# Two causal blocks instead of four in an FFT convolution that runs beside a feed-forward layer

## The chip, the cores and the metric

The kernel runs on one core of a Trainium2 chip. The metric is the device time of one execution in microseconds (us). TensorE multiplies matrices into PSUM; VectorE (DVE), ScalarE (ACT) and GpSimd (POOL) work elementwise, and GpSimd works from SBUF alone in this kernel; SyncE (SP) issues nearly all DMAs.

## The reference, cut to what matters

```python
# x, v: (2, 12480, 128)   pos_emb: (12480, 64)   w_in: (128, 2048)   w_out: (2048, 128)
h = (relu(pos_emb @ w1) @ w2) * exp(-0.01 * pos)      # the filter, one per channel
u = x * v
y = irfft(rfft(u, n=2*S, axis=1) * rfft(h, n=2*S, axis=0), n=2*S, axis=1)[:, :S]   # causal convolution
z = (x * y).reshape(24960, 128)
a = z @ w_in
out = maximum(0.01 * a, a) @ w_out
```

## The kernel before, in words

The sequence is cut into NBLK = 4 causal blocks of 3136 tokens. A *unit* (b, j) is block j of batch b; the eight units run in the order (0,0), (1,0), (0,1), (1,1), and so on to (1,3). Batch 0 also carries the filter: its units transform 64 more channels (`hid`), so they do more work.

Each unit has a **forward stage** (`ConvA`) and an **inverse stage** (`ConvB`). The forward stage loads tokens, multiplies x by v on GpSimd (`prep`, L198), makes a first Fourier step on TensorE (`burst`, L224), copies PSUM to SBUF (ACT, L169; only in the first unit half of them on DVE, L646) and stores that to DRAM (`scr1`). The inverse stage goes through chunks of frequencies (NCH = 7 per unit): it loads a chunk (`bin`), makes the second Fourier step (`up`, L400; `ep` L352 and `hp` L381 for the filter), multiplies spectra, sums the products into `pin`, and transforms back (`dp`, L436) into `scr2`. `up` and `burst` share one PSUM buffer of two banks (`cv`) once the feed-forward layer runs, so each use of `cv` waits until the elementwise engine has emptied it.

Block j of the output needs the products of block spectra u(i)·g(j-i). With half-shifted spectra in this kernel, block j costs 1, 2, 5 and 2 chunk products for j = 0, 1, 2, 3 (`first` runs on DVE from PSUM, L416; `rest` runs on GpSimd from SBUF, L416 too; `join`, L424 to L426, adds and subtracts them on GpSimd, for j = 2 partly on DVE). That makes ten per batch. Both engines' products use the same two buffers `t0` and `t1`.

The **feed-forward layer** runs in 52 tiles of up to 490 tokens. A tile has 16 steps; a step is three matmuls with `w_in` (`m1`, L765 to L767), ACT and DVE work that makes two parts of the activation (`rh` L771, `rl` L772), and three matmuls with `w_out` (`m2`, L789 to L792). In front of a tile stand `front` calls (L744 `yp`, DVE `zt` L746, transposes): they finish the convolution for 4 token groups and make z. There are 64 of them.

The first unit (0,0) runs alone, before the layer starts, mixed with the unpacking of the weights (`wprep`, a generator that is advanced 4 or 3 times per step of `ConvB`). We call that part the **head**. Every engine takes its instructions in the order of the program. The order after the head is set by `pace`: each unit gets a window of feed-forward steps, sized by the table `cost`, and the pieces of its two stages are spread evenly over the window:

```python
cost = [0, 80, 110, 110, 215, 215, 125, 125]      # weight of each unit after the first
self.rest = {0: [], 1: [(u(0), g(1), "y")], 3: [(u(0), g(3), "y")],
             2: [(u(1), g(1), "y"), (u(1), g(2), "p"), (u(0), g(2), "y")]}[j]
```

Units must be done before the first `front` that needs them. Tiles after the last unit use another activation path (`k >= LEAKY`) that has three matmuls fewer per tile and more ACT and DVE work.

## Time and profile before

| | |
|---|---|
| time, median of 3 runs | 2028.54 us (2026.91 to 2029.88) |
| profiled execution, its own time | 2025.03 us |
| its span, first to last instruction | 2023.2 us |
| TensorE busy | 1760.4 us, 87% |
| VectorE, ScalarE, GpSimd busy | 45%, 40%, 45% |
| mean granted TensorE clock | 0.949 |
| DMA | 290.54 MB, mean 144 GB/s |

TensorE is the busiest engine by far. The 45% of GpSimd is a mean over the whole span, and its work is bunched: in the forty slices of the page it is at 7 to 8 tenths in some slices and at 1 or 2 in others. The granted clock is the share of full speed (2.4 GHz) that TensorE was given; the lower of its two levels is half of that, so a mean of 0.9 over a stretch says that it had the lower level for a fifth of the stretch.

### The profile page before, as it was taken

Reading aid. Unit: us, or ns where it says so; the run is one execution under the profiler, and the core shown is the slowest. Engines: PE = TensorE matmul, PEld = TensorE weight load, DVE = VectorE, ACT = ScalarE, POOL = GpSimd, SP = SyncE. Lnnn points to the kernel's source line nnn. Section 1 sums busy time; section 2 is a strip of 40 time slices with the busy share of each in tenths; the row PEclk is TensorE's granted clock in tenths of the full one; section 3 lists DMA queues with packets and bytes.
Section 4 is the critical chain, followed back from the end, with each engine's and each line's share of the span. In section 5 each row is a group of like instructions: output and inputs, shape, how many; then the busy total and the mean of one; then the engine's idle time right before and its main releaser. Section 6 shows DMA issues by size and latency. Waiting matters only on the chain.

```text
span 2023.2 us, 27361 instructions
## 1 busy us (share of the span) xinstructions
PE 1760.4 (87%) x9932; PEld 1302.7 (64%) x9932; DVE 901.2 (45%) x1435; ACT 819.1 (40%) x1459; POOL 901.6 (45%) x608
## 2 busy tenths in 40 slices
PE   3765989978998899787889878789989999999999
PEld 2433846755675577555568656567766687668888
DVE  3763443333443434433444444444333444445665
ACT  1222534533453354232235323234543354335666
POOL 4221121157418610888772388882148622860000
PEclk9976989999999999888989998899999999999999
DMA  6547664566565555354335443333556355631110
GB/s 147 161 135 235 177 194 137 141 236 209 151 182 192 175 146 176 122 162 133 126 89 132 148 145 132 117 99 103 145 193 223 112 144 171 192 115 56 40 32 16
DMA packets 203935, 290.54 MB, mean 144 GB/s; under 512 B 26503, under 2 KB 135017, under 8 KB 203605
## 3 DMA queue, kind: packets, MB, share of 16 engines
q1 hardware_dynamic: 200098, 286.57, 46.8%
q10 hardware_dynamic: 3703, 2.24, 0.6%
q8 instruction: 78, 1.28, 0.3%
q14 instruction: 56, 0.46, 0.1%
HBM read 181.23 MB, written 107.51 MB: 143 GB/s over the span
## 4 chain that ended last, share of the span: by engine, by line
PE 58%; POOL 20%; DVE 8%; issue 7%; DMA 3%; ACT 2%; SPq 1%; ACTq 0%; POOLq 0%; DVEq 0%
POOL t L416 10%; PE mh L765 8%; PE mh L767 6%; PE mh L766 6%; PE acc L790 6%; PE acc L792 6%; PE acc L789 6%; PE cv L224 4%; POOL t L424 4%; PE cv L400 4%; DVE t L416 3%; PE cv L436 3%; PE yp L744 2%; POOL pin L425 2%; POOL pin L426 2%
## 5 line engine op out<-in xcount | busy, mean ns | idle before, releaser
L772 DVE SCALAR_TENSOR_TENSOR rl<-mh,rh 128x490 fp32r<-128x490 f32 (+3 forms) x704 | 458.8, 662 | 603.7 <-ACT rh L771 601.7
L771 ACT ACTIVATE rh<-mh 128x490 fp32r<-128x490 f32 (+3 forms) x704 | 406.4, 579 | 503.1 <-PE mh L767 483.7
L765 PE MATMUL mh<-zh,w_in_h 128*128 128x490 f32 (+4 forms) x832 | 367.1, 441 | 66.9 <-DVE rl L772 66.2
L766 PE MATMUL mh<-zl,w_in_h 128*128 128x490 f32 (+4 forms) x832 | 323.4, 389 | 0.0
L767 PE MATMUL mh<-zh,w_in_l 128*128 128x490 f32 (+4 forms) x832 | 323.2, 389 | 0.0
L790 PE MATMUL acc<-rl,w_out_h 128*128 128x490 f32 (+4 forms) x832 | 321.8, 387 | 0.0
L789 PE MATMUL acc<-rh,w_out_h 128*128 128x490 f32 (+4 forms) x832 | 321.0, 386 | 0.0
L792 PE MATMUL acc<-rh,w_out_l 128*128 128x490 f32 (+4 forms) x832 | 320.9, 386 | 0.0
L765 PEld LDWEIGHTS mh<-zh,w_in_h 128*128 128x128 f32 x832 | 161.5, 194 | 195.1 <-DVE rl L772 92.0
L425 POOL TENSOR_TENSOR pin<-t,t 128x512 f32<-128x512 f32 (+1 forms) x112 | 142.4, 1272 | 258.8 <-DVE t L416 250.8
L416 DVE TENSOR_TENSOR t<-cv,sp 128x1024 f32<-128x1024 f32 (+1 forms) x126 | 133.8, 1103 | 112.0 <-POOL pin L426 67.8
L416 POOL TENSOR_TENSOR t<-sp 128x1024 f32<-128x1024 f32 (+1 forms) x84 | 178.1, 2141 | 9.6 <-issue 6.9
L767 PEld LDWEIGHTS mh<-zh,w_in_l 128*128 128x128 f32 x832 | 161.8, 194 | 27.4
L789 PEld LDWEIGHTS acc<-rh,w_out_h 128*128 128x128 f32 x832 | 161.7, 194 | 26.7
L792 PEld LDWEIGHTS acc<-rh,w_out_l 128*128 128x128 f32 x832 | 160.8, 193 | 26.5
L790 PEld LDWEIGHTS acc<-rl,w_out_h 128*128 128x128 f32 x832 | 160.3, 193 | 27.0 <-DVE rl L780 0.2
L766 PEld LDWEIGHTS mh<-zl,w_in_h 128*128 128x128 f32 x832 | 163.5, 196 | 13.5 <-DVE zl L758 0.3
L198 POOL TENSOR_TENSOR t<-pp,ct 113x512 f32<-113x512 f32 x28 | 36.1, 1290 | 202.5 <-PE cv L224 93.1
L400 PE MATMUL cv<-bin,mb 128*64 128x512 f32 (+1 forms) x416 | 109.4, 638 | 17.2 <-ACT hs L386 12.6
L416 POOL TENSOR_TENSOR t<-sp,hs 128x1024 f32<-128x1024 f32 (+1 forms) x56 | 118.8, 2143 | 7.4 <-issue 4.6
L436 PE MATMUL cv<-pin,mi 64*128 64x512 f32 (+1 forms) x416 | 109.3, 631 | 14.2 <-DVE t L416 13.1
L424 POOL TENSOR_TENSOR t<-t,pin 128x1024 f32<-128x1024 f32 (+1 forms) x56 | 119.5, 2134 | 0.0
(123 smaller groups left out, 1886.3 us busy)
## 6 DMA issues: line engine op xcount, KB each, us to landing
sp<-g SPq DMA_DIRECT2D x72, 512.0 KB
cin<-scr SPq DMA_DIRECT2D x64, 392.0 KB
scr<-ct SPq DMA_DIRECT2D x96, 256.0 KB
sp<-u SPq DMA_DIRECT2D x48, 512.0 KB
scr<-sp SPq DMA_DIRECT2D x64, 294.0 KB
bin<-scr SPq DMA_DIRECT2D x24, 768.0 KB
scr<-sp SPq DMA_DIRECT2D x32, 392.0 KB
g<-hs SPq DMA_DIRECT2D x24, 512.0 KB
```

Source lines behind the costliest of these rows:

```text
L400: nc.tensor.matmul(p[64 * jo:64 * jo + 64, ri, :w].rearrange("p (k d) -> p k d", d=D), mb[:, ri, :], t[:, jo * h:jo * h + h, self.off:], s ...
L416: eng.tensor_tensor(out=t[i], in0=u[:R, :, :w], in1=g[:R, i:i + 1, :w].to_broadcast([R, 2, w]), op=ALU.mult)
L424: G(out=t[0], in0=t[0], in1=init[:R, :, :w], op=ALU.add)
L425: G(out=acc[:R, 0, :w], in0=t[0][:, 0], in1=t[1][:, 1], op=ALU.subtract)
L765: nc.tensor.matmul(hp, w_in_h[:, fs], zh, start=True, stop=False)
L766: nc.tensor.matmul(hp, w_in_h[:, fs], zl, start=False, stop=False)
L767: nc.tensor.matmul(hp, w_in_l[:, fs], zh, start=False, stop=True)
L771: nc.scalar.activation(out=rh, in_=hp, func=AF.Relu)
L772: nc.vector.scalar_tensor_tensor(out=rl, in0=hp, scalar=0.0, in1=rh, op0=ALU.max, op1=ALU.subtract)
L789: nc.tensor.matmul(ap, w_out_h[:, f, :], rh, start=(f == 0), stop=False)
L790: nc.tensor.matmul(ap, w_out_h[:, f, :], rl, start=False, stop=False)
L792: nc.tensor.matmul(ap, w_out_l[:, f, :], rh, start=False, stop=last and k >= LEAKY)
```

## The change

The sequence is cut into two blocks of 6272 tokens. A block has twice as many rows in the forward transform; these are paired with their neighbours half a block apart, so that the transform matrices stay as small as before and a sum and a difference (a radix-2 butterfly) join the two halves. Four things follow.

- The forward stage ends a burst with one ACT copy of one half and two DVE operations (sum, difference) instead of one ACT copy of both halves. A unit has twice as many bursts.
- An inverse chunk covers 4 frequencies of both halves instead of 8 of one. A unit has 13 chunks instead of 7. Block 0 costs one product and block 1 two, three per batch. DVE's products get buffers of their own (`sp3` and `pp`), GpSimd keeps `t0` and `t1`.
- Before a `front`, GpSimd joins the two halves of `cin` (`join_front`, two operations of 98x512). The table `gt` of the last inverse step, formerly resident in SBUF, is loaded for each front into a ring of two.
- There are four units. The first one, still in the head, is twice as large. `wprep` starts later in the forward stage and is advanced 3 or 2 times per step in the inverse stage. `cost` has three entries.

```diff
-NBLK = 4
+NBLK = 2
-BLK = KA * NM
+BLK = KA * NB
-KC = 8
+KC = 4
...
             def burst(self, c, i0, n):
...
-                self.evac(turn[0], o, a[:, :, :n * e].rearrange("k w (i e) -> k w i e", e=e))
+                a1 = cpt("a1s", 512, 2)[:2 * KA, :n * e]
+                nc.scalar.copy(a1, a[:, 1, :n * e])
+                a0, a1 = (t.rearrange("k (i e) -> k i e", e=e) for t in (a[:, 0, :n * e], a1))
+                nc.vector.tensor_tensor(out=o[:, :, 0, :], in0=a0, in1=a1, op=ALU.add)
+                nc.vector.tensor_tensor(out=o[:, :, 1, :], in0=a0, in1=a1, op=ALU.subtract)
...
-                self.first = [(g(0), "y")] + ([(g(1), "p")] if j == 2 else [])
-                self.rest = {0: [], 1: [(u(0), g(1), "y")], 3: [(u(0), g(3), "y")],
-                             2: [(u(1), g(1), "y"), (u(1), g(2), "p"), (u(0), g(2), "y")]}[j]
-                self.loads = [("p", b)] if j == 3 else []
+                self.first = [(g(0), "y")]
+                self.rest = [] if j == 0 else [(u(0), g(1), "y")]
+                self.loads = []
...
-                if self.j < 2:
+                if self.j == 0:
                     us = self.tile("us", 1024).rearrange("p (r w) -> p r w", r=2)
                     nc.scalar.copy(us[:R, :, :w], p[:R, :, :w])
...
-            def t01(self, c):
+            def t01(self, c, fresh):
                 R, w = self.dims(c)
-                return [cpt(f"t{i}", 1024).rearrange("p (r w) -> p r w", r=2)[:R, :, :w] for i in range(2)]
+                t = (spt(3), cpt("pp", 1024)) if fresh else (cpt("t0", 1024), cpt("t1", 1024))
+                return [i.rearrange("p (r w) -> p r w", r=2)[:R, :, :w] for i in t]
...
         def load_front(t):
...
+            g = gr()
+            for r in range(2):
+                nc.sync.dma_start(out=g[KA * r:KA * r + KA, :NI * 2 * KA].rearrange("k (i n) -> k i n", n=2 * KA),
+                                  in_=cg[:KA, m0 % 32:m0 % 32 + NI, r, m0 // 32, 0, :])
...
+        def join_front(t):
+            c, g, xt = mlp_in[t]
+            cj = fr.tile([128, 2, NI, D], F32, tag="cj", name="cj", bufs=1)[:2 * KA]
+            eng = nc.gpsimd if t else nc.vector
+            for p, op in ((0, ALU.add), (1, ALU.subtract)):
+                eng.tensor_tensor(out=cj[:, p], in0=c[:, :, 0, :], in1=c[:, :, 1, :], op=op)
+            mlp_in[t] = cj, g, xt
...
-                load_t(NI, 16 - NI, (nc.sync, nc.scalar))
+                load_t(NI, 32 - NI, (nc.sync, nc.scalar))
...
-                for _ in range(4 if i < 7 else 3):
+                for _ in range(3 if i < 7 else 2):
                     next(wprep, None)
...
-        cost = [0, 80, 110, 110, 215, 215, 125, 125]
+        cost = [0, 220, 310, 290]
...
         for t in range(1, total):
+            at(ends[t] - 7, "join", t)
             at(ends[t] - 3, "front", t)
             at(ends[t], "front", t)
```

**DVE in the forward stage of unit (1,0).** This is VectorE's queue at the start of the feed-forward layer (`rl` is the layer's own work, `zt` and `zl` belong to a front, `cv` is the PSUM of a burst). Before:

```order
L772 SCALAR_TENSOR_TENSOR rl<-mh,rh 128x392 x2
L746 TENSOR_TENSOR zt<-yp,xm_108 113x512
L772 SCALAR_TENSOR_TENSOR rl<-mh,rh 128x392 x3
L758 TENSOR_TENSOR zl<-zp,zh 128x392
L772 SCALAR_TENSOR_TENSOR rl<-mh,rh 128x392 x5
L746 TENSOR_TENSOR zt<-yp,xm_107 113x512
```

Now:

```order
L792 SCALAR_TENSOR_TENSOR rl<-mh,rh 128x392 x5
L756 TENSOR_TENSOR zt<-yp,xm_90 113x512
L237 TENSOR_TENSOR sp<-cv,a1s 98x4x128
L238 TENSOR_TENSOR sp<-cv,a1s 98x4x128
L792 SCALAR_TENSOR_TENSOR rl<-mh,rh 128x392 x3
L778 TENSOR_TENSOR zl<-zp,zh 128x98
L778 TENSOR_TENSOR zl<-zp,zh 128x294
L792 SCALAR_TENSOR_TENSOR rl<-mh,rh 128x392 x2
```

The two rows on `cv` and `a1s` are the butterfly. They are new on DVE, and the PSUM buffer is free for TensorE's next use only after the second.

**GpSimd in an inverse chunk.** Before, one chunk of unit (1,2), the block with five products (`sp` are loaded spectra, `t_` are `t0` and `t1`, `pin` and `pp` are the two sums):

```order
L425 TENSOR_TENSOR pin<-t_9154,t_9155 128x512
L426 TENSOR_TENSOR pin<-t_9154,t_9155 128x512
L425 TENSOR_TENSOR pp<-t_9215,t_9216 128x512
L426 TENSOR_TENSOR pp<-t_9215,t_9216 128x512
L416 TENSOR_TENSOR t_9237<-sp 128x1024
L416 TENSOR_TENSOR t_9238<-sp 128x1024
L424 TENSOR_TENSOR t_9237<-t_9237,pin 128x1024
L425 TENSOR_TENSOR pin<-t_9237,t_9238 128x512
L416 TENSOR_TENSOR t_9292<-sp 128x1024
L416 TENSOR_TENSOR t_9293<-sp 128x1024
L424 TENSOR_TENSOR t_9292<-t_9292,pp 128x1024
L425 TENSOR_TENSOR pp<-t_9292,t_9293 128x512
```

Four more rows of the same kind (a third product) follow before the next chunk. Now, one chunk of unit (1,1), the second of its thirteen, and the join that follows it:

```order
L438 TENSOR_TENSOR pin<-sp,pp 128x512
L439 TENSOR_TENSOR pin<-sp,pp 128x512
L429 TENSOR_TENSOR t_11459<-sp 128x1024
L429 TENSOR_TENSOR t_11460<-sp 128x1024
L437 TENSOR_TENSOR t_11459<-t_11459,pin 128x1024
L438 TENSOR_TENSOR pin<-t_11459,t_11460 128x512
L439 TENSOR_TENSOR pin<-t_11459,t_11460 128x512
L584 TENSOR_TENSOR cj<-cin 98x512 x2
```

A unit of batch 0 has two operations of 128x256 more in each chunk. The join `cj` is new in this queue, behind whatever of the chunk is not yet done.

**SyncE at a front.** The loads of one front before:

```order
L566 DMA cin<-scr_01_70 98x2x512
L95 DMA xm_107<-in_x_dram 48x512 x2
L98 DMA xm_107<-in_x_dram 2x512
```

And now:

```order
L569 DMA cin<-scr_10_65 98x1024
L573 DMA gt_94<-in_cg_dram 49x4x98 x2
L92 DMA xm_90<-in_x_dram 48x512 x2
L95 DMA xm_90<-in_x_dram 2x512
```

The two `gt` loads are new in SP's queue at each of the 64 fronts.

## Rows read from the trace of the kernel before

**Rows 1.** Windows by stage: sum, busy per engine, granted clock, DMA share, GB/s

```profile
core 0: us, PE busy (x) PEld busy (x) DVE busy (x) ACT busy (x) POOL busy (x), PEclk, DMA share, GB/s
0.00:192.80 192.80, 104.83 (x643) 62.65 (x643) 98.28 (x183) 45.12 (x79) 58.43 (x64) 0.87 0.58 163
192.80:255.00 62.20, 62.20 (x400) 51.40 (x401) 25.35 (x43) 28.71 (x50) 7.65 (x6) 0.92 0.67 192
255.00:325.00 70.00, 59.51 (x250) 34.32 (x250) 28.25 (x36) 26.07 (x42) 15.86 (x14) 0.93 0.59 181
325.00:395.00 70.00, 65.91 (x411) 50.24 (x411) 26.90 (x45) 33.97 (x61) 10.28 (x8) 1.00 0.52 141
395.00:525.00 130.00, 109.96 (x738) 75.17 (x735) 45.68 (x63) 52.00 (x84) 81.90 (x58) 0.96 0.63 206
...
590.00:702.00 112.00, 98.04 (x457) 64.24 (x457) 46.49 (x67) 42.43 (x72) 76.37 (x49) 0.97 0.60 192
...
795.00:1055.00 260.00, 206.70 (x1155) 148.65 (x1154) 107.86 (x159) 80.73 (x144) 204.55 (x122) 0.89 0.42 131
...
1125.00:1375.00 250.00, 205.90 (x932) 151.84 (x931) 114.27 (x172) 78.12 (x144) 195.34 (x108) 0.90 0.38 119
...
1480.00:1610.00 130.00, 118.04 (x788) 80.36 (x785) 52.43 (x73) 48.39 (x83) 99.96 (x70) 0.99 0.55 181
...
1695.00:1815.00 120.00, 112.37 (x554) 79.79 (x551) 55.83 (x82) 43.16 (x79) 91.57 (x56) 0.97 0.51 159
1815.00:2023.20 208.20, 201.41 (x1107) 172.03 (x1106) 124.98 (x231) 129.45 (x255) 0.00 (x0) 1.00 0.13 37
```

**Rows 2.** Waits of DVE in the inverse stage of unit (1,1): total us, times, longest

```profile
DVE t L416 <- POOL pin L426: 30.2, 6, 6.7
```

**Rows 3.** Timeline of TensorE in the head: start us, duration us

```profile
32.98 1.60 PE L224 MATMUL cv<-t,tt 49*98 49x192 f32 x8
37.74 1.60 PE L224 MATMUL cv<-t,tt 49*98 49x192 f32 x8
69.22 4.52 PE L224 MATMUL cv<-t,tt 49*98 49x192 f32 x24
94.43 3.27 PE L400 MATMUL cv<-bin,mb 128*64 128x512 f32 x8
154.54 3.68 PE L400 MATMUL cv<-bin,mb 128*64 128x512 f32 x8
163.91 1.94 PE L400 MATMUL cv<-bin,mb 128*64 128x512 f32 x8
192.76 0.69 PE L765 MATMUL mh<-zh,w_in_h 128*128 128x392 f32 x1 [0.57 <-ACT zh L757]
```

**Rows 4.** Groups of instructions by line: count, busy us, mean ns, idle before

```profile
L416 POOL TENSOR_TENSOR t<-sp 128x1024 f32<-128x1024 f32 (+1 forms) x84 | 178.1, 2141 | 9.6 <-issue 6.9
L425 POOL TENSOR_TENSOR pin<-t,t 128x512 f32<-128x512 f32 (+1 forms) x112 | 142.4, 1272 | 258.8 <-DVE t L416 250.8 <-PE mh L767 2.5
L416 DVE TENSOR_TENSOR t<-cv,sp 128x1024 f32<-128x1024 f32 (+1 forms) x126 | 133.8, 1103 | 112.0 <-POOL pin L426 67.8 <-ACT us L404 31.6 <-PE cv L400 10.9
L169 ACT COPY sp<-cv 98x768 f32<-98x768 f32 (+1 forms) x80 | 70.9, 886 | 74.5 <-PE cv L224 68.7 <-DMA scr<-sp 3.2 <-DMA out_dram<-os 1.8
L746 DVE TENSOR_TENSOR zt<-yp,xm 113x512 f32<-113x512 f32 x64 | 44.1, 689 | 35.8 <-PE yp L744 33.7 <-DMA e<-es 0.4 <-DMA hs<-in_v_dram 0.4
L400 PE MATMUL cv<-bin,mb 128*64 128x512 f32 (+1 forms) x416 | 109.4, 638 | 17.2 <-ACT hs L386 12.6 <-ACT hs L388 3.7 <-DVE t L416 1.0
L436 PE MATMUL cv<-pin,mi 64*128 64x512 f32 (+1 forms) x416 | 109.3, 631 | 14.2 <-DVE t L416 13.1 <-POOL pin L425 1.0
L224 PE MATMUL cv<-t,tt 49*98 49x128 f32 (+3 forms) x1024 | 104.1, 336 | 2.0 <-ACT pts L207 1.2 <-DVE t L213 0.6
L381 PE MATMUL cv<-w,esg 64*64 64x128 f32 x588 | 25.4, 296 | 0.0
L352 PE MATMUL cv<-mb,bin 128*64 128x128 f32 x294 | 25.0, 312 | 45.6 <-issue 41.8 <-DMA bin<-scr 2.3 <-DVE t L416 1.5
```

More of the change, by code (lines that the diff above doesn't have):

```diff
@@ L166, in __init__ @@
                 self.off = self.e - D
-                self.granules = granules or [(8 * i, 8) for i in range(4)]
+                self.granules = granules or [(8 * i, 8) for i in range(8)]
                 self.alloc = alloc or self.shared
-                self.evac = evac or (lambda n, o, a: nc.scalar.copy(o, a))
                 self.got, self.uh, self.late = [], {}, []
@@ L174, in shared, with load @@
                 return cpt(tag, 512 if kind == "p" else 1024)
-            def load(self, q=None, only="pxv"):
-                q = q or {}
+            queues = {}
+            def load(self):
+                q = self.queues
                 g = len(self.got)
@@ L715, in tile_conv_mlp @@
         psc["bank"] = psc["single"] = lambda: psc["pair"]()[:, :512]
-        total = 8 * len(UNITS)
-        size = [2 * NI * rows_of(UNITS[t // 8][1]) for t in range(total)]
+        total = FT * len(UNITS)
+        size = [NI * (rows_of(UNITS[t // FT][1], 0) + rows_of(UNITS[t // FT][1], 1)) for t in range(total)]
         groups = [(t, i) for t in range(total) for i in range(NI)]
@@ L721, in tile_conv_mlp @@
         tiles = [groups[a:b] for a, b in zip([0] + cuts, cuts + [len(groups)])]
-        widths = [sum(size[t] // NI for t, _ in g) for g in tiles]
+        real = [sum(size[t] // NI for t, _ in g) for g in tiles]
+        widths = [w + w % 2 for w in real]
         NTL = len(tiles)
-        assert sum(widths) == B * S
+        assert sum(real) == B * S
         z, acc, ots = {}, {}, {}
@@ L735, in front @@
         def front(t):
-            u = UNITS[t // 8]
-            rows, i0 = rows_of(u[1]), t % 8 * NI
-            c, xt = mlp_in.pop(t)
+            j = UNITS[t // FT][1]
+            rows = [rows_of(j, p) for p in range(2)]
+            c, g, xt = mlp_in.pop(t)
             yp = ps.tile([128, 512], F32, tag="io", name="yp")
             for i in range(NI):
-                for w in range(2):
-                    g = gt[:2 * KA, (i0 + i) * 2 * KA + w:(i0 + i) * 2 * KA + w + 127:2]
-                    nc.tensor.matmul(yp[64 * w:64 * w + 64, i * D:i * D + D], g, c[:, w, i, :], start=True, stop=True)
+                for p in range(2):
+                    nc.tensor.matmul(yp[64 * p:64 * p + 64, i * D:i * D + D],
+                                     g[:2 * KA, i * 2 * KA + p:i * 2 * KA + p + 127:2], c[:, p, i, :],
+                                     start=True, stop=True)
             zt = sm.tile([128, NI, D], F32, tag="zt", name="zt", bufs=1)
@@ L754, in front @@
                     z[k] = [sm.tile([128, WIDE], F32R, tag=g, name=g, bufs=ZB) for g in ("zh", "zl")]
-                zh, zl = (i[:, a:a + m * 2 * rows].rearrange("p (i w a) -> p i w a", w=2, a=rows) for i in z[k])
-                src = zp[:, i0:i0 + m].rearrange("p i (w a) -> p i w a", w=2)[:, :, :, :rows]
-                nc.scalar.copy(zh, src)
-                nc.vector.tensor_tensor(out=zl, in0=src, in1=zh, op=ALU.subtract)
+                n = sum(rows)
+                zh, zl = (i[:, a:a + m * n].rearrange("p (i n) -> p i n", n=n) for i in z[k])
+                src = zp[:, i0:i0 + m].rearrange("p i (w a) -> p i w a", w=2)
+                if rows[0] == rows[1]:
+                    cuts_ = [(src[:, :, :, :rows[0]], *(o.rearrange("p i (w a) -> p i w a", w=2) for o in (zh, zl)))]
+                else:
+                    cuts_ = [(src[:, :, w, :rows[w]], *(o[:, :, KA * w:KA * w + rows[w]] for o in (zh, zl)))
+                             for w in range(2)]
+                if a + m * n == real[k] < widths[k]:
+                    h, l = (i[:, real[k]:widths[k]] for i in z[k])
+                    cuts_.append((zp[:, 0, :1], h, l))
+                for q, h, l in cuts_:
+                    nc.scalar.copy(h, q)
+                    nc.vector.tensor_tensor(out=l, in0=q, in1=h, op=ALU.subtract)
         def m1(k, f):
@@ L836, in tile_conv_mlp @@
         ends[0] = 0
-        dead = [0] + [ends[8 * n] - 16 for n in range(1, len(UNITS))]
+        dead = [0] + [ends[FT * n] - 16 for n in range(1, len(UNITS))]
         LEAKY = (dead[-1] + 8) // NF + 1
-        cost = [0, 80, 110, 110, 215, 215, 125, 125]
+        cost = [0, 220, 310, 290]
         def windows(scale):
@@ L896, in do @@
             if what == "conv":
-                while done[0] < upto[t // 8]:
+                while done[0] < upto[t // FT]:
                     step()
@@ L901, in do @@
                 load_front(t)
+            elif what == "join":
+                join_front(t)
             elif t in fronts:
```

282 lines of the change are left out of this document (135 added, 147 removed).

## The prediction, made before the changed kernel ran

> **What bounds the kernel now.** I read the windows by stage first [rows 1], because a mean over the span hides where TensorE waits. Each row gives TensorE's busy time and the granted clock. What a stage loses is its idle time (sum minus PE busy) plus the time given away at a lower clock, (1 - clock) x sum. The reader is to see four kinds of stage. The head, 0 to 192.8 us, has TensorE busy for 104.8 us only. The forward stages lose almost nothing: 0 + 5.0 us in the stretch 192.8 to 255, 4.1 us in 325 to 395, and 2.5 us in all in the four stretches between the rows shown. The inverse stages lose 15.4 us for unit (1,0), 25.2 for (0,1), 17.3 for (1,1), 81.9 for (0,2), 69.1 for (1,2), 13.3 for (0,3) and 11.2 for (1,3). The tail after 1815 us loses 6.8. Together 251.7 us behind the head, 174.8 of idle time and 76.9 of clock. So TensorE's own work behind the head is 2023.2 - 192.8 - 251.7 = 1578.7 us; I call this the floor.
>
> The two worst stages are those with five products. GpSimd is busy there for 204.6 of 260 and 195.3 of 250 us: it is the limit, and TensorE waits and drops to its lower clock. Next I asked who holds whom in a stage with two products. In unit (1,1) DVE's product waits 30.2 us for GpSimd to let go of the shared buffers `t0` and `t1`, up to 6.7 us at a time [rows 2]; while DVE stands, the layer's `rl` queues behind it and TensorE runs out of `mh` buffers.
>
> **The change, part by part.**
>
> *Products.* Before, ten per batch x 7 chunks x 2 batches = 140 chunk products; now three x 13 x 2 = 78, of the same size (128x1024). On GpSimd 70 products become 26. One costs two multiplies at 2.14 us, a sum of the same size, and two adds at 1.27 us [rows 4]. The stages with five products vanish, and their 151 us of loss with them. What comes in their place is priced below.
>
> *TensorE's work.* The number of columns in `burst`, `ep`, `hp`, `up` and `dp` is the same in total, since blocks are twice as long and half as many. But one more pass of a batch-0 unit moves from behind the head into it. Its price by group sums [rows 4]: `burst` 15.6 us (104.1 us are four pairs of units at 192 and 128 channels: 104.1/4 x 0.6), `up` and `dp` 13.7 each (an eighth), `ep` and `hp` 8.3 and 8.5 (a third of the three units behind the head), and about 5 for the filter's small matmuls, for which no row stands here. That makes 65 us. New floor: 1578.7 - 65 = 1514 us. I leave out six tiles that lose three matmuls each, a few us.
>
> *Head, forward stage.* 16 bursts took from 32.98 to 73.7 us [rows 3], 2.55 us each. Now there are 32. Each burst costs ACT half of the 0.89 us copy and DVE two operations. The nearest row for those is `zt` (113x512, PSUM and SBUF in, 0.69 us) [rows 4]; at 384 columns I take 0.5 us each, 1.0 against 0.5 us per burst before. TensorE stays the limit, so I take 2.7 us per burst: 86 us. ACT issues more DMAs before its first copy and between copies: +6 us. The transform table's second load grows from 12 to 28 rows. The third burst, which needs it, ran directly behind the second at 37.74 us, so its delay was nothing before; the load was issued at about 18 us. If landing scales with rows it comes at up to 18 + 20 x 28/12 = 65 us, at best with no delay; I take 12 us. Last burst done at 33 + 6 + 12 + 86 = 137 us (bounds 118 and 155).
>
> *Head, inverse stage.* From the last burst to the first `up` 21 us [rows 3]; now 19, as the weights advance 21 steps instead of 28 there. A chunk took (154.54 - 94.43)/4 = 15.0 us while weights were unpacked at 12 steps per chunk, and 163.91 - 154.54 = 9.4 us at the end of that. At 8 steps per chunk I take 9.4 + 5.6 x 8/12 = 13.1 us for six intervals and 9.4 for five: 126 us (bounds 11 x 9.4 = 103 and 11 x 15.0 = 165). From the last full `up` to the layer's first matmul 28.9 us, as before: stores, loads and the front are the same, and the first join is 1.3 us. The layer starts at 137 + 19 + 126 + 29 = 311 us instead of 192.8 (bounds 275 and 365). So the head grows by 118 us, of which 65 come back from the floor.
>
> *Losses behind the head.* The first stretch keeps 5 us. For the inverse stages I use how thinly the pieces are spread (feed-forward steps per piece, from the planner's windows), against loss per chunk [rows 1]: in batch-0 units 3.6 us at 0.84 steps and 1.9 at 1.09; in batch-1 units 2.5 at 1.30 and 1.6 at 1.83. Now the two-product units have 1.42 and 2.1 steps per piece, GpSimd's chunk (11.5 us, 12.9 with the filter) is as long as in the old two-product units but there are about 8.6 steps per chunk instead of 5, and DVE no longer shares buffers with it. I take 1.5 us x 13 = 20 and 1.3 x 13 = 17. Unit (1,0) lost 2.2 us per chunk at 1.25 steps, because its `dp` waits for DVE's product in the one `cv` buffer; at 2.2 steps I take 0.5 x 13 = 7. If the cover is gone, the old 2.2 to 3.6 stay.
>
> *Butterflies.* A burst holds `cv` for ACT's half copy (0.5 us) and two DVE operations (1.0 to 1.4) instead of 0.9 us, about 1 us more, hidden by the 1.4 to 2.2 steps that lie between pieces. The old forward stage of (0,1) lost 4.1 us over 16 bursts; I take 8 for 32 bursts, and 2 for the 16 of (1,1). Bounds: nothing, and the full hold of 2.1 us on all 64 bursts.
>
> *Joins.* 63 joins on GpSimd at 2 x 1.27 us are 160 us of an engine that gave up more than that. They are issued four steps ahead of their front. In a forward stage or the tail GpSimd is idle and the join costs nothing. In a two-product chunk it can stand behind 5 to 7 us of products; about 16 fronts fall there, 0.6 us each: 10 us (bounds nothing and 16 x 7 = 112). The `gt` loads have about 18 steps of lead; nothing.
>
> *Tail.* 6.8 becomes 10, as it is longer and has more ACT and DVE work. TensorE is busy for 97% of it now.
>
> Sum of losses: 5 + 7 + 8 + 20 + 2 + 17 + 10 + 10 = 79 us (bounds 40 and 160).
>
> **Sum.** 311 + 1514 + 79 = 1904 us of span. The profiled execution's own time lay 1.8 us above its span and 3.5 us below the median of the runs shown: 1904 + 1.8 + 3.5, about 1910 us, 5.8% below 2028.5.
>
> **The rivals.**
>
> 1. *The head takes it back.* Loads of many short runs are slow, ACT's issuing delays its copies, chunks stay at 15 us: layer start at 365 us, 1963 us in all. The transform table alone, landing at 65 us and not near 45, would give 1920. For it: the head's DMA share is 0.58 already [rows 1]. Against: the last chunk interval of 9.4 us. The Trainium skill, DMA: Bandwidth & Descriptors, section "Why a DMA increments its semaphore by 16 and not by 1", says that a DMA runs on the largest number of engines up to 16 that divides its outer dimension. By that rule the table's loads of 49 rows get 7 engines, which speaks for the late landing; no trace here shows the spread.
> 2. *The inverse stages keep their loss per chunk.* (25.2 + 17.3)/14 = 3.0 us x 26 chunks = 79 instead of 37: 1952 us. For it: PE stalled in them at 1.3 steps per piece. Against: (0,3) lost 1.9 per chunk with GpSimd busy for 100 of 130 us [rows 1].
> 3. *Slower: the butterfly stalls every burst.* If each of the 64 bursts behind the head made TensorE wait its full hold of 2.1 us, and clock were lost with it at the ratio of the rows (76.9 to 174.8), the loss is 64 x 2.1 x 1.44 = 194 us: 2094 us. It decides from 118/(64 x 1.44) = 1.3 us per burst. Against: `cv` was held 0.9 us per burst before and 16 bursts lost 4.1 us in all.
> 4. *The relief does not come.* Losses behind the head stay near 200 us although products go: about 2031 us. Against: all but 100 us of the loss lies in the two stages that vanish.
> 5. *Better.* Head at 285 us, losses 45 us: 1850 us.
>
> **How the numbers follow.** The forecast, 1865 to 1950 us, 0.62; rival 1 0.14; rival 2 0.10; rival 3 0.05; rival 4 0.02; rival 5 0.07. Predicted 1910 us. The range runs from 1865 to 1980: it takes in rivals 1 and 2 and leaves out 3, 4 and most of 5. Faster by more than 0.2% (about what a measurement of this kernel can tell from no change): 0.62 + 0.14 + 0.10 + 0.07 = 0.93; within 0.2%: 0.01; slower: 0.06.
>
> **What the profile after would show.** The layer's first `mh` matmul at 275 to 365 us, the last head burst near 137 us, head chunks falling from 13 to 9.4 us. Behind the head TensorE's idle and clock loss together near 79 us, no stretch of 250 us below 0.95 clock, GpSimd at 6 to 8 tenths in the two-product stages, and DVE's waits for `pin` gone. A layer start beyond 365 us, waits of `yp` for `cj` of more than 3 us each, or a `burst` that waits for DVE each time would make the prediction wrong.

## The result and the profile after

The changed kernel takes 1843.39 us (median of 3 runs, 1842.28 to 1843.57) against 2028.54 us before: ratio 0.9086, 95% interval 0.9066 to 0.9107. It is faster, by 9.1% where 5.8% were forecast, and 22 us below the low end of the range. The profiled execution took 1843.57 us with a span of 1841.8 us.

The windows by stage after, with the columns of [rows 1]. In order: the head; the forward and the inverse stage of unit (1,0); of (0,1); of (1,1); the tail.

```profile
core 0: us, PE busy (x) PEld busy (x) DVE busy (x) ACT busy (x) POOL busy (x), PEclk, DMA share, GB/s
0.00:288.80 288.80, 173.91 (x1217) 101.66 (x1217) 139.99 (x270) 77.87 (x135) 94.92 (x102) 0.85 0.66 196
288.80:430.00 141.20, 139.04 (x899) 115.48 (x900) 80.27 (x131) 62.81 (x118) 36.76 (x29) 0.98 0.55 147
430.00:605.00 175.00, 168.98 (x826) 112.44 (x825) 84.84 (x117) 76.96 (x128) 43.75 (x37) 1.00 0.62 182
605.00:810.00 205.00, 201.47 (x1175) 156.75 (x1174) 115.92 (x204) 92.42 (x183) 41.94 (x34) 1.00 0.44 124
810.00:1080.00 270.00, 260.29 (x1718) 184.29 (x1716) 117.90 (x167) 112.78 (x195) 187.40 (x134) 1.00 0.56 170
1080.00:1240.00 160.00, 157.18 (x1001) 129.16 (x998) 90.14 (x155) 74.39 (x150) 40.67 (x32) 1.00 0.55 145
1240.00:1460.00 220.00, 217.97 (x1089) 156.79 (x1087) 115.13 (x180) 91.71 (x181) 168.09 (x105) 1.00 0.56 169
1460.00:1841.80 381.80, 370.06 (x2004) 313.89 (x2002) 242.79 (x457) 237.22 (x496) 45.48 (x37) 0.99 0.17 45
```

Read as before, idle time plus clock, the stretches behind the head lose 5.0, 6.0, 3.5, 9.7, 2.8, 2.0 and 15.6 us: 44.6 us in all, where the kernel before lost 251.7. TensorE's floor is 1841.8 - 288.8 - 44.6 = 1508.4 us. The clock has two digits only, so the split between floor and losses is good to a few us. The span fell by 181.4 us, and the three terms give it: head +96.0 (288.8 against 192.8), floor -70.3, losses -207.1.

TensorE's timeline in the head after, with the columns of [rows 3]; the first and last burst, the first and last full `up`, the layer's first matmul:

```profile
33.52 1.60 PE L229 MATMUL cv<-t,tt 49*98 49x192 f32 x8
...
131.36 1.60 PE L229 MATMUL cv<-t,tt 49*98 49x192 f32 x8
...
148.69 2.62 PE L412 MATMUL cv<-bin,mb 128*64 128x512 f32 x8
...
256.67 1.94 PE L412 MATMUL cv<-bin,mb 128*64 128x512 f32 x8
...
288.79 0.69 PE L785 MATMUL mh<-zh,w_in_h 128*128 128x392 f32 x1 [0.57 <-ACT zh L777]
```

The eleven intervals between the twelve full `up` take 108.0 us, 9.8 each.

Groups by line after, with the columns of [rows 4]: the joins, GpSimd's two multiplies and its sum of a product, one of its adds, and the butterfly's first operation on DVE.

```profile
L584 POOL TENSOR_TENSOR cj<-cin 98x512 f32<-98x512 f32 x126 | 161.2, 1301 | 353.8 <-issue 193.0 <-PE yp L752 123.4 <-DMA cin<-scr 31.4
L429 POOL TENSOR_TENSOR t<-sp 128x1024 f32<-128x1024 f32 (+1 forms) x26 | 58.4, 2270 | 0.0
L437 POOL TENSOR_TENSOR t<-t,pin 128x1024 f32<-128x1024 f32 (+1 forms) x26 | 58.6, 2255 | 0.0
L438 POOL TENSOR_TENSOR pin<-t,t 128x512 f32<-128x512 f32 (+1 forms) x26 | 31.8, 1222 | 2.0
L237 DVE TENSOR_TENSOR sp<-cv,a1s 98x384 f32<-98x384 f32 (+1 forms) x96 | 57.8, 602 | 83.9 <-ACT a1s L235 82.8 <-DMA xm<-in_x_dram 0.7 <-DMA x<-in_x_dram 0.3
```

TensorE's waits behind the head after: in total us, times, longest.

```profile
PE op L843 <- DVE zl L778: 18.2, 12, 2.1
PE cv L363 <- issue: 6.2, 6, 1.0
PE cv L448 <- DVE pp L429: 4.8, 8, 0.8
PE mh L785 <- DVE rl L792: 1.4, 2, 1.0
PE cv L208 <- DVE sp L238: 0.9, 4, 0.3
PE cv L215 <- DVE sp L238: 0.8, 4, 0.2
...
```

Three things are to be seen. The butterfly (`sp` L238) holds TensorE for 1.7 us in all, so 64 bursts cost next to nothing. Behind the head no `yp` waits for a join. And `mh` waits for `rl` 1.4 us; in the kernel before that wait was the largest, 66.2 us in 32 times:

```profile
PE mh L765 <- DVE rl L772: 66.2, 32, 4.9
```

### The profile page after: what moved, and what is told of

Read it like the earlier page. It is cut to its first block, busy times and chain, and to the rows that moved or that the text cites. A ratio compares the mean times of both kernels' runs of the same rounds, so it can differ in the third digit from the quotient of the medians.

```text
span 1841.8 us, 27676 instructions
## 1 busy us (share of the span) xinstructions
PE 1688.9 (92%) x9914; PEld 1270.5 (69%) x9914; DVE 987.0 (54%) x1678; ACT 826.2 (45%) x1583; POOL 659.0 (36%) x506
## 4 chain that ended last, share of the span: by engine, by line
PE 82%; DVE 4%; DMA 3%; ACT 2%; issue 2%; SPq 1%; ACTq 0%; DVEq 0%
PE mh L785 12%; PE mh L787 9%; PE acc L809 9%; PE acc L812 9%; PE acc L810 9%; PE mh L786 9%; PE cv L448 5%; PE cv L412 4%; PE cv L229 4%; PE yp L752 3%; PE op L843 2%; DMA bin<-scr 2%; PE cv L393 1%; PE zp L761 1%; DVE pp L429 1%
## 5 line engine op out<-in xcount | busy, mean ns | idle before, releaser
L792 DVE SCALAR_TENSOR_TENSOR rl<-mh,rh 128x490 fp32r<-128x490 f32 (+2 forms) x608 | 399.7, 663 | 432.0 <-ACT rh L791 431.3
L791 ACT ACTIVATE rh<-mh 128x490 fp32r<-128x490 f32 (+2 forms) x608 | 350.2, 579 | 381.6 <-PE mh L787 340.5
L785 PE MATMUL mh<-zh,w_in_h 128*128 128x486 f32 (+3 forms) x832 | 348.9, 419 | 1.9 <-DVE rl L792 1.4
L812 PE MATMUL acc<-rh,w_out_l 128*128 128x486 f32 (+3 forms) x832 | 316.0, 380 | 0.0
L787 PE MATMUL mh<-zh,w_in_l 128*128 128x486 f32 (+3 forms) x832 | 315.9, 380 | 0.0
L809 PE MATMUL acc<-rh,w_out_h 128*128 128x486 f32 (+3 forms) x832 | 315.8, 380 | 0.0
L786 PE MATMUL mh<-zl,w_in_h 128*128 128x486 f32 (+3 forms) x832 | 315.8, 380 | 0.0
L810 PE MATMUL acc<-rl,w_out_h 128*128 128x486 f32 (+3 forms) x832 | 315.6, 379 | 0.0
L584 POOL TENSOR_TENSOR cj<-cin 98x512 f32<-98x512 f32 x126 | 161.2, 1301 | 353.8 <-issue 193.0
L800 DVE TENSOR_TENSOR rl<-sp,rh 128x486 fp32r<-128x486 f32 (+1 forms) x224 | 152.4, 685 | 74.2 <-ACT rh L799 70.0
L786 PEld LDWEIGHTS mh<-zl,w_in_h 128*128 128x128 f32 x832 | 157.8, 190 | 14.4 <-DVE zl L778 0.3
```

Of the source, the lines that this page charges most:

```text
L584: eng.tensor_tensor(out=cj[:, p], in0=c[:, :, 0, :], in1=c[:, :, 1, :], op=op)
L785: nc.tensor.matmul(hp, w_in_h[:, fs], zh, start=True, stop=False)
L786: nc.tensor.matmul(hp, w_in_h[:, fs], zl, start=False, stop=False)
L787: nc.tensor.matmul(hp, w_in_l[:, fs], zh, start=False, stop=True)
L791: nc.scalar.activation(out=rh, in_=hp, func=AF.Relu)
L792: nc.vector.scalar_tensor_tensor(out=rl, in0=hp, scalar=0.0, in1=rh, op0=ALU.max, op1=ALU.subtract)
```

## The experiments

Two questions were open: why the losses fell further than forecast, and what the head is made of. For the first, theory S (slack) says that a chunk's chain of work on DVE and GpSimd now has enough feed-forward steps to hide behind. Its rival D says that DVE's own product buffers did it. For the second, W says that unpacking the weights on DVE holds the head's chunks, its rival M that memory traffic does. "Steps" are feed-forward steps of the layer.

| run | us, median | ratio to before, 95% interval | layer starts at |
|---|---|---|---|
| changed kernel | 1843.39 | 0.9086 [0.9066, 0.9107] | 288.8 |
| shared_t | 1842.75 | 0.9096 [0.9083, 0.911] | 288.8 |
| dense | 1932.84 | 0.9531 [0.9507, 0.9555] | 289.2 |
| dense_shared | 1955.92 | 0.9641 [0.9614, 0.9669] | 289.0 |
| before_own_t | 1998.82 | 0.9865 [0.9849, 0.9881] | 193.1 |
| before_fewer | 1882.11 | 0.928 [0.9262, 0.9298] | 192.2 |
| before_fewer_even | 1837.12 | 0.9057 [0.9042, 0.9072] | 191.0 |
| extra1 (one run) | 1947.09 | | 281.0 |
| extra2 (one run) | 2154.32 | | 283.8 |
| weights_first | 1859.74 | 0.9187 [0.9163, 0.9211] | 303.7 |
| more_saves | 1850.63 | 0.9139 [0.9113, 0.9164] | 292.2 |
| early_ct | 1830.01 | 0.9038 [0.9017, 0.9059] | 273.5 |
| early | 1831.01 | 0.9021 [0.9008, 0.9035] | 275.5 |
| wf_bin3 | 1878.48 | 0.9261 [0.9246, 0.9277] | 320.1 |
| early_bin3 | 1857.78 | 0.916 [0.9146, 0.9174] | 303.0 |
| wf_bin3u4 | 1848.53 | 0.9115 [0.91, 0.9131] | 292.7 |
| early_bin3u4 | 1825.17 | 0.8999 [0.8985, 0.9012] | 269.6 |
| early_bin3u4ct | 1822.87 | 0.8986 [0.8972, 0.8999] | 264.8 |

### Buffers and pace

**shared_t**: the changed kernel, both engines' products in `t0` and `t1` again.

```diff
-                t = (spt(3), cpt("pp", 1024)) if fresh else (cpt("t0", 1024), cpt("t1", 1024))
+                t = (cpt("t0", 1024), cpt("t1", 1024))
```

> The changed kernel, with DVE's products back in the two buffers that GpSimd uses. Theory S (slack): the inverse stages lose little now because a chunk of 11.7 us on GpSimd has some 17 to 21 us of feed-forward and convolution matmuls around it; buffers matter little: 1843 to 1856 us. Theory D (decoupling): DVE's own buffers took the loss away; sharing brings back 2 to 3 us for each of the 26 two-product chunks: about 1895 us, with DVE waiting for pin again for tens of us.

**dense**: the changed kernel with each unit's pieces in the last 0.59 of its window, which is about the old 5 steps per chunk in place of 8.6.

```diff
                 s, e = max(0, knots[n - 1]), knots[n]
+                s = e - 0.59 * (e - s)
```

> The changed kernel, with the pieces of each unit squeezed into the last 59% of its window, about 5 feed-forward steps per two-product chunk as before the change instead of 8.6. Own buffers stay. Theory S: GpSimd's chunk no longer fits, loss per chunk returns to 2.5 to 3.6 us, about 26 x 2.5 = 65 us more: 1900 us or more. Theory D: 1843 to 1856 us.

**dense_shared**: both edits.

> The kernel after at the dense pace of the old order, and with the two shared product buffers for both engines. It fills the fourth field of a square: pace thin or dense, buffers own or shared (1843 own and thin, 1843 shared and thin, 1933 own and dense). If sharing costs only where pieces stand close (26 us for 42 such products in the kernel before, here there are 26 with a product on GpSimd behind them), the time is 1933 + 16 to 40, so 1949 to 1973 us. Rival: in the changed kernel sharing never matters, since DVE's products are ten steps apart also then: 1928 to 1940 us.

**before_own_t**: the kernel before, with a spare spectrum buffer and `pp` for DVE's products in every block but the third, which needs `pp`.

```diff
-                return [cpt(f"t{i}", 1024)... for i in range(2)]
+                t = (spt(4), cpt("pp", 1024)) if fresh else (cpt("t0", 1024), cpt("t1", 1024))
...
-                t = self.t01(c)
+                t = self.t01(c, eng is nc.vector and self.j != 2)
```

> The kernel before, with buffers of their own for DVE's products in all units but those of block 2 (blocks 1 and 3 lost 25.2 + 17.3 + 13.3 + 11.2 = 67 us). Theory D: half of these 67 us goes: 1995 us. Theory S: at most 8 us goes: 2020 to 2029 us.

Sharing alone costs nothing (1842.75); packing the same pieces closely costs 89 us (1932.84); both, another 23 (1955.92). So D is wrong where pieces are thin, and right as a second effect where they are dense: in the kernel before own buffers take 26 us off. The rows that carry this are DVE's waits for GpSimd's last add. In order, behind the head: the kernel before, before_own_t (where all lines are one further), dense_shared.

```profile
DVE t L416 <- POOL pin L426: 67.8, 24, 6.7
```

```profile
DVE t L417 <- POOL pin L427: 9.2, 9, 1.6
```

```profile
DVE t L429 <- POOL pin L439: 69.2, 16, 6.7
```

In shared_t this wait is almost gone, as GpSimd has mostly let go of the buffers before DVE asks:

```profile
DVE t L429 <- POOL pin L439: 3.9, 2, 2.5
```

Four windows of dense show the stages in which TensorE idles again: the inverse stage of (1,0), the forward stage of (0,1), and the inverse stages of (0,1) and (1,1). The two rows below are the last two stages in dense_shared.

```profile
492.00:626.00 134.00, 116.84 (x531) 66.36 (x528) 56.89 (x74) 49.69 (x76) 40.83 (x34) 0.95 0.69 205
626.00:946.00 320.00, 294.86 (x1645) 233.26 (x1645) 156.86 (x266) 131.91 (x256) 49.77 (x40) 0.96 0.36 102
946.00:1160.00 214.00, 189.05 (x1290) 124.52 (x1287) 79.69 (x106) 75.31 (x123) 179.17 (x127) 0.97 0.60 186
1397.00:1573.00 176.00, 161.92 (x766) 104.92 (x763) 80.88 (x121) 60.26 (x114) 160.50 (x101) 0.97 0.61 190
```

```profile
946.00:1169.00 223.00, 190.87 (x1297) 125.99 (x1294) 79.42 (x106) 75.36 (x123) 179.46 (x127) 0.96 0.57 179
1405.00:1600.00 195.00, 169.21 (x769) 107.44 (x768) 80.48 (x121) 60.58 (x115) 161.33 (x101) 0.94 0.56 172
```

Idle time plus clock, the four stages of dense lose 23.9, 37.9, 31.4 and 19.4 us, where the changed kernel lost 6.0, 3.5, 9.7 and 2.0. So the forward stage of (0,1) loses more than either stage with two products, and GpSimd is busy there for 49.8 of 320 us: its throughput can't be the cause in that stage. In the last two stages it is busy for 84% and 91%. In dense_shared these two lose 41.1 and 37.5 us, 3.2 and 2.9 per chunk, about what the prediction read from the old stages of (0,1) and (1,1), 3.6 and 2.5: with the old pace and the old buffers the old loss is back. TensorE's waits behind the head in dense, some of the list:

```profile
PE cv L363 <- issue: 15.3, 9, 2.6
PE cv L448 <- DVE pp L429: 14.4, 10, 3.1
PE yp L752 <- POOL cj L584: 9.6, 7, 3.4
PE cv L215 <- DVE sp L238: 8.6, 10, 1.8
PE cv L412 <- ACT hs L398: 5.5, 4, 1.7
```

In the changed kernel the first was 6.2 us (it is `ep`, and the profile names no releaser for it); each of the others was under 5 us, or not in the list: `dp` behind DVE's product in the one `cv` buffer (all of it in the inverse stage of (1,0)), the joins (8.8 of the 9.6 us in that of (1,1)), the butterflies (in the forward stage of (0,1)), the filter's copy. Many small waits appear together where there is too little work of the layer between the pieces. That pace makes the loss is shown; how much of it in the last two stages is GpSimd's share and how much these short waits, no run separates.

### The number of products

**extra1, extra2**: the changed kernel with one or two more products per two-product chunk on GpSimd, whose result is thrown away. Each is followed by a sum and two adds.

```diff
+                        for _ in range(1):          # extra2: range(2)
+                            t = self.mult(c, nc.gpsimd, vals[u], vals[g])
+                            yield
+                            nc.gpsimd.tensor_tensor(out=t[0], in0=t[0], in1=t[1], op=ALU.add)
+                            for k in range(2):
+                                nc.gpsimd.tensor_tensor(out=t[k][:, 0], in0=t[k][:, 0], in1=t[k][:, 1], op=ALU.add)
+                            yield
```

> The changed kernel with one more product in each two-product chunk, whose result is thrown away (two multiplies, one sum of the same size, two half-size adds, 9.2 us on GpSimd; the two pieces more also give the inverse stage a larger share of its window, so that a chunk gets 9.8 and 10.1 steps). Theory S: GpSimd then needs 24.0 us per chunk of unit (0,1) against 22.4 us on TensorE and 22.6 against 18.9 for (1,1): 21 + 48 us of idle time and some lower clock, about 1925 us. Rival (TensorE loses time per dependent piece, not through GpSimd's share): below 1860 us.

> As extra1 with two products more per chunk, thrown away (four products per chunk, near the five of block 2 before). Theory S: GpSimd needs 33.3 and 31.9 us per chunk against 23.6 and 20.3 us on TensorE: 126 + 150 us of idle time and lower clock with it, 2120 to 2200 us. Rival (loss per piece): below 1880 us.

One more costs 103 us of span, a second another 207. Behind the head, where these products run, it is 111 and 204 us, since the layer started 8 and 5 us earlier in these two executions. The first came out 22 us above the time that was expected; the second lies in its band. Most of the price can be read off the windows of the changed kernel, a reckoning made after the runs. GpSimd's free time in its two inverse stages is 270 - 187.4 + 220 - 168.1 = 134.5 us, or 5.2 us per chunk. The extra product takes 2 x 2.27 + 2.26 + 2 x 1.22 = 9.2 us in each of 26 chunks, 239 us. So the first should add 239 - 134.5 = 104.5 us, and adds 111. The second should add 239 and adds 204. Waits of `yp` for the joins, then, in extra1 and in extra2, and a window of the inverse stage of (0,1) in extra1 (POOL, the fifth busy time, 301.84 of 320):

```profile
PE yp L759 <- POOL cj L591: 45.7, 17, 10.4
```

```profile
PE yp L759 <- POOL cj L591: 145.4, 34, 19.9
```

```profile
810.00:1130.00 320.00, 280.69 (x1714) 194.94 (x1712) 119.67 (x171) 113.72 (x198) 301.84 (x196) 0.95 0.44 135
```

This is the wait of the joins that the prediction feared. It is large only where GpSimd is nearly full, at 94% in this window; it was 9.6 us in dense and nothing in the changed kernel.

**before_fewer**: the kernel before, with two products in place of five in the third block and without the sum `p` for the fourth; it leaves out part of the convolution. **before_fewer_even**: the same, with windows for the third block like its neighbours'.

```diff
-                self.first = [(g(0), "y")] + ([(g(1), "p")] if j == 2 else [])
+                self.first = [(g(0), "y")]
...
-                             2: [(u(1), g(1), "y"), (u(1), g(2), "p"), (u(0), g(2), "y")]}[j]
+                             2: [(u(0), g(2), "y")]}[j]
...
-        cost = [0, 80, 110, 110, 215, 215, 125, 125]
+        cost = [0, 80, 110, 110, 110, 110, 125, 125]      # before_fewer_even alone
```

> The kernel before, with four blocks, its short head and its table of windows, but with two products in place of five in the third block, whose result is therefore incomplete, and without the sum p that the fourth block would add. The windows stay, so those two units have about twice as many steps per piece. If the products on GpSimd and the pace make the loss, the 151 us of the two stages fall to 10 to 25: 1885 to 1905 us. Rival: the loss comes from something that four blocks have and two have not (more units, their stores and loads), and the products matter little: above 1960 us.

> As before with the third block cut to two products, and its two windows cut from 215 to 110, so that all the other units get windows 1.24 times as wide. If pace sets the loss, the 58 us that units (1,0), (0,1) and (1,1) lost fall by half and the third block loses as much as its neighbours, 8 to 12 us per unit: 20 to 40 us below the run with the old windows, 1850 to 1880 us. Rival: the loss of a chunk is set by its products whatever the pace: the same time as with the old windows within 10 us.

The stretch behind the head, of before_fewer and of before_fewer_even:

```profile
193.00:1878.70 1685.70, 1609.17 (x9289) 1215.47 (x9289) 760.73 (x1182) 774.77 (x1380) 570.81 (x404) 0.98 0.46 138
```

```profile
193.00:1831.70 1638.70, 1590.44 (x9286) 1204.54 (x9285) 760.10 (x1182) 775.89 (x1380) 570.84 (x404) 1.00 0.48 142
```

Idle time falls from 174.8 us (worked out in the prediction from [rows 1]) to 76.5, and to 48.3 once the freed windows are spread over all units. Four blocks with two products then take 1837 us, about as long as the new kernel with its two blocks and its radix-2 work. Both parts of S hold: the products made 147 us of the loss (2029.6 - 1882.1), the pace in the other units 45 more (1882.1 - 1837.1); the first time is 3 us below its band and the second 13, a gain of 45 us for the 20 to 40 expected. This version computes less than the reference and is no kernel to use; it shows where the gain of the change comes from.

### The head

**weights_first**: three steps of `wprep` per tile in the head's forward stage from tile 30 on, in place of one. **more_saves**: the head stores `u` twice, 512 KB more per chunk.

```diff
                     if i >= 30:
                         next(wprep, None)
+                        next(wprep, None)          # weights_first
+                        next(wprep, None)
...
                     self.save(("u", self.b, self.j), c, us)
+                    if self.defer is not None:     # more_saves
+                        self.late.append(lambda: nc.sync.dma_start(out=self.dram(("x", 0), c), in_=us[:R, :, :w]))
```

> The changed kernel with the weights unpacked three steps per piece in the head's forward stage, so that none is left for its inverse stage. Theory W (weights hold the head's chunks): the seven intervals of 10.6 us fall to 8.5, 15 us off the inverse stage, and the forward stage grows by about as much, as DVE works there then: within 6 us of 1843. Theory M (DMA holds the chunks): intervals stay near 9.8 us on average, the forward stage grows by 15 us: about 1858 us.

> The changed kernel with one more store of 512 KB in each chunk of the head's inverse stage (the spectrum u a second time, to memory that nobody reads). Theory M (DMA holds the chunks at 250 to 278 GB/s): 512 KB at 270 GB/s are 1.9 us in each of 12 chunks, the layer starts about 20 us later: 1863 us. If something else holds the chunks: within 5 us of 1843.

The second store adds 5 us to the eleven intervals (113.1 against 108.0), not the 20 of M, so M is not the rule; the time is 7 us longer, just outside the band of the other theory. With the weights out of the way the intervals fall to 85.9 us, 7.8 each, but the forward stage grows by 39 us where 15 were expected. So the time of weights_first comes out as M had it, for a reason that M does not give. W and M are both incomplete, as the `up` rows of weights_first show:

```profile
192.47 1.94 PE L412 MATMUL cv<-bin,mb 128*64 128x512 f32 x8
198.35 1.94 PE L412 MATMUL cv<-bin,mb 128*64 128x512 f32 x8
...
227.72 1.94 PE L412 MATMUL cv<-bin,mb 128*64 128x512 f32 x8
238.81 1.94 PE L412 MATMUL cv<-bin,mb 128*64 128x512 f32 x8
245.00 1.94 PE L412 MATMUL cv<-bin,mb 128*64 128x512 f32 x8
255.95 1.94 PE L412 MATMUL cv<-bin,mb 128*64 128x512 f32 x8
```

A chunk takes 5.8 us where nothing holds it, and 11 in every second place. TensorE waits there for the loaded chunk:

```profile
PE s L363 <- DMA bin<-scr: 24.4, 7, 9.2
```

**early** sends the weights' first loads out ten tiles earlier; **early_ct** also gives the last inverse step's copy (`ct`) a ring of three in the head.

```diff
-                    if i >= 30:
+                    if i == 20 or i >= 30:
...
-                ct = cpt("ct", KC * 2 * D).rearrange(...)
+                ct = (cpt("ct", KC * 2 * D) if self.defer is None else spt(c % 3)).rearrange(...)      # early_ct
```

> The changed kernel with the first weight loads issued ten pieces earlier in the head, and three buffers in turn for the head's inverse results (ct). In the profile DVE waits 7.0 us for the first weights while TensorE and ACT stand for 7.2 and 4.1 us, and ACT waits 12.4 us in all for the store of ct. If these waits are on the path that sets the layer's start: 10 to 16 us off, 1828 to 1834 us. If DMA sets the start: within 4 us of 1843.

> The kernel after, with one edit of the two in the run early_ct: the weights' first loads go out ten tiles earlier in the head, the buffer of the last inverse step stays single. If both edits gave their part, this one gives 5 to 10 of the 13 us: 1833 to 1839 us. Rival: all of it came from the buffer: 1841 to 1845 us; or all of it from the loads: 1828 to 1832 us.

Both are faster than the changed kernel, and as far as these runs can tell all of it comes from the loads: early alone has 0.9021. What it removes is a stall in the forward stage. DVE's and then TensorE's timeline of the changed kernel:

```profile
82.72 0.29 DVE L120 TENSOR_SCALAR fa<-wi 128x256 uint32<-128x256 uint32 x1 [6.98 <-DMA wi<-in_moe_w_in_dram]
```

```profile
86.11 0.64 PE L208 MATMUL s<-ident,p 113*128 113x113 f32 x2 [7.24 <-DVE t L217]
92.40 1.20 PE L215 MATMUL s<-w1bd,pts 128*113 128x128 f32 x4 [4.11 <-ACT pts L211]
```

DVE stands 7 us before the unpacking of a weight that has not landed, and the work behind it in the queue, butterflies among it, stands too; TensorE's second wait follows from the first. In early this wait is gone, the last burst starts at 123.42 us and not at 131.36. That is 8 of the 13 us by which the layer starts earlier. The other 5 lie behind the forward stage, and I have no cause for them.

**wf_bin3, early_bin3**: weights_first and early with a third buffer for `bin` in the head (`self.deep` is 1 in the head's unit and 0 in the others). To make room, `u` gets three buffers instead of four. **wf_bin3u4, early_bin3u4** give `u` its fourth buffer back, in one that idles in the head; **early_bin3u4ct** has two buffers for `ct` as well.

```diff
-                    t = cpt("bin", KC * 2 * C0, 2)[...]
+                    t = (self.tile("bin", KC * 2 * C0) if self.deep and c % 3 == 2 else cpt("bin", KC * 2 * C0, 2))[...]
...
-                            self.load_bins(c + 2)
+                            self.load_bins(c + 2 + self.deep)
...
-                return hb.tile([128, n], F32, tag=tag, name=tag, bufs=4)
+                return hb.tile([128, n], F32, tag=tag, name=tag, bufs={"bin": 1, "us": 3}.get(tag, 4))
...
-                    us = self.tile("us", 1024)
+                    us = (spt(0) if self.deep and c % 4 == 3 else self.tile("us", 1024))      # u4
```

> The run weights_first with a third buffer for the loaded chunk (bin) in the head, so that its load goes out one chunk earlier; the buffers of the saved spectra u go from four to three to make room. In weights_first the first Fourier step of the filter waited 24.4 us in seven chunks for bin, and chunks took 5.8 and 11 us in turn. If the latency of that load was the limit, the chunks all take 5.8 to 6.5 us, the layer starts 18 to 24 us earlier and the time is 1836 to 1844 us. Rival: the memory moves no faster, and the wait goes to the saves and to the loads one chunk on: 1852 to 1862 us.

> The run early with the same third buffer for bin in the head. There the waits for bin were 10.5 us in four chunks, and weights are unpacked beside the chunks. If each of the two holds its own share, 5 to 10 us go: 1821 to 1826 us. Rival: the unpacking on DVE holds the chunks and fills the gap: 1828 to 1833 us.

> As wf_bin3, but the fourth buffer of the saved spectra u is given back, in a buffer that is idle in the head. wf_bin3 had no more waits for bin in the chunks but one, and 53 us of waits of ACT's copy of u for the save of an earlier u. If those waits were the missing buffer's, the chunks now take 5.8 to 7 us each and the layer starts at 280 to 288 us: 1836 to 1846 us. Rival: the memory is the limit in the head, the loads and saves of a chunk take what they take, and the wait only changes its place: 1855 to 1880 us.

> As early_bin3, with the fourth buffer of u given back. If the missing buffer cost the 27 us and the earlier load of bin helps beside the weights, 1820 to 1828 us. If the unpacking on DVE holds the chunks, 1828 to 1834 us. If the memory is the limit, 1835 us or more.

> As early_bin3u4, with two buffers for the last inverse step in the head as well. Waits of its copy for the store were 10 to 12 us in three or four chunks. If chunks are held by single late buffers, 2 to 8 us below early_bin3u4; if by the unpacking or the memory, the same within 3 us.

The first pair was a miss in both theories: 19 and 27 us slower. The waits for `bin` went to one, but ACT's copy of `u` now waited for the save of an earlier `u`; the row is of wf_bin3.

```profile
ACT us L417 <- DMA u<-us: 53.3, 9, 6.4
```

With the fourth buffer back that wait is gone, and the chunks of wf_bin3u4 run as expected at first:

```profile
192.20 1.94 PE L413 MATMUL cv<-bin,mb 128*64 128x512 f32 x8
198.07 1.94 PE L413 MATMUL cv<-bin,mb 128*64 128x512 f32 x8
203.84 1.94 PE L413 MATMUL cv<-bin,mb 128*64 128x512 f32 x8
```

The eleven intervals are 74.5 us, 6.8 each; the first five take 5.4 to 5.9 us, the other six 6.5 to 8.9, and ACT waits 38.6 us for the store of the single `ct`. The time, 1848.5 us, is 11 below weights_first but 2.5 above the expected band. That the single `ct` buffer now held the chunks is likely; no run tries a second one with this order of the weights. Beside the weights the third `bin` buffer brings 5.8 us in the medians (1831.0 to 1825.2), with intervals of the ratios that overlap. The second `ct` buffer's 2.3 us are within what these runs can tell. early_bin3u4ct has the lowest time of all, 1822.87 us. One reservation: extra1 and extra2 have the same code in the head as the changed kernel and yet started the layer 8 and 5 us earlier. I have no cause for that, so differences of that size in a head, seen in one profile, prove nothing by themselves.

## Why the prediction was right and wrong

**Right.** The direction and its reason: the head grows, the floor falls, and the five-product stages go with their loss. before_fewer shows it alone, 147 us where the sum had 151. The floor was 1508.4 for 1514; 4 of the 6 us are the six tiles left out of the sum, with three matmuls each less. (A row of such a matmul lasts 0.38 us, but rows overlap: the three of one tile begin at 712.55, 712.77 and 712.99 us, so one costs 0.22 us.) The butterflies cost no more than was forecast: (0,1) lost 3.5 us and (1,1) 2.8 in their forward stages, where 8 and 2 were taken. One operation took 0.56 us at the 384 columns for which 0.5 was taken (the 0.60 of the row mixes in those at 512 columns), and it is hidden. A slip of reading changes nothing: the 2.5 us between the rows shown are five stretches, not four.

**Right by luck.** The head's forward stage ended at 133.0 for 137. The first burst began at 33.52 us, so next to nothing of the 6 us for ACT's issues showed, and the 12 us for the larger table were 0. In their place stood two waits that the sum did not have, 7.24 and 4.11 us of TensorE behind a weight that landed late. Without them a burst took (99.4 - 11.4)/32 = 2.75 us, where 2.7 was taken.

**Wrong: losses behind the head, 79 forecast and 44.6 measured (-34 of the 62 us of span).** The step that failed is the loss per chunk of the two-product stages, 1.5 and 1.3 us, taken from old stages by steps per piece. The mechanism, pace, was right; the size of its term was not. Measured are 9.7/13 = 0.75 and 2.0/13 = 0.15. The old rows came from stages with about 5 steps per chunk and with buffers that both engines shared. I had noted that there are now 8.6 steps and no sharing, but did not count with it. The experiments put both back: at 5 steps the same chunks lose 31.4/13 = 2.4 and 19.4/13 = 1.5 us (dense), with the shared buffers as well 3.2 and 2.9 (dense_shared), and the shared buffers alone add nothing (shared_t). The whole of dense, 1933 us, is more than these two stages: 39 of its 92 us behind the head are theirs.

It isn't the steps alone that cover GpSimd's chunk of 11.7 us (2 x 1.23 + 2 x 2.27 + 2.26 + 2 x 1.22): the six matmuls of a step begin 0.22 us apart (one step begins at 705.79 us, the next at 707.11), so a step is 1.3 us and 8.6 are 11.3 us. The matmuls of the chunk itself and of the fronts lie there too, and TensorE is busy for 260.3/13 = 20.0 and 218.0/13 = 16.8 us per chunk, GpSimd, joins included, for 14.4 and 12.9.

The joins were priced at 10 us and cost 0: 5.2 us per chunk are free on GpSimd. They wait in dense (9.6 us), most of it where GpSimd is busy for 91% of the stage, and in extra1 (45.7 us). The tail was taken too low, 15.6 us for 10; 7.8 of it are TensorE's waits for DVE's `zl` there.

**Wrong: the head's inverse stage, 126 forecast and 108.0 measured (-18).** The sum took 13.1 us per chunk with weights and 9.4 without. Measured are 10.6 for the first seven and 8.45 for the last four, and 5.8 where neither weights nor a late `bin` hold a chunk. The base of 9.4 us came from one interval of the kernel before, which was itself held: its `up` took 3.68 us where the next took 1.94 [rows 3], and DVE unpacked a weight at its start (L120 to L131, 153.90 to 157.30 us). It is not the price of a chunk. The pieces around it were 3.3 us shorter before the first `up` and 3.1 longer behind the last.

**The rivals.** The fifth (head at 285, losses 45, 1850 us) is what happened, with a chance of 0.07. Its condition was met to 4 us in the head and to 0.4 in the losses. It gave no mechanism for either number, so this is a hit of two numbers and not of an account. The first has nothing for it: the head's third burst, which needs the larger table, began at 38.29 us, right behind the second. The rule of the Trainium skill that stood beside it (DMA: Bandwidth & Descriptors, section "Why a DMA increments its semaphore by 16 and not by 1") is neither shown nor refuted by that, since no view here tells the engines of one load. The second's 3.0 us per chunk come back with the old pace and the old buffers (dense_shared). The third's mechanism has 1.7 us in the changed kernel; at the pace of dense TensorE's waits for the butterflies (L208 and L215 behind `sp` L238) grow to 12.9 us. The fourth was refuted by the windows.

## What to carry to other kernels

When work is spread between another layer's steps, compare for each engine the time of one round of it with the time of the steps that lie between, and read the free time from the busy column of the stage: it came within 7 us of what one more product costs, and was 35 us too high for the second. A loss per round that was measured at a close pace can't be scaled to a wide one. Rows of matmuls that overlap can't be added up to a time: take the distance between their starts. Before a buffer is taken from one ring for another, look how late the ring's last user is; and a load that an in-order engine needs between critical work belongs well ahead of it.

## What the runs showed of the hardware

GpSimd's 128x1024 operation costs the same before and after: taken by shape, 2.37 to 2.38 us in the kernel before and 2.38 to 2.40 us in the changed one. The means of the groups, 2.14 us in [rows 4] and 2.26 above, differ because each unit's last chunk is narrower ("+1 forms") and is one of seven before and one of thirteen now. The granted clock was 0.98 to 1.00 in the changed kernel's stages behind the head, where TensorE is busy for 96% and more, and 0.94 to 0.97 in the rows of dense and dense_shared above, where it is busy for 86 to 92%. Idle time is not all of it: in the first stretch behind the head of the kernel before the clock was 0.92 with TensorE busy throughout [rows 1].
